# Three edits to a fused attention and two-expert-layer kernel: a written instruction order in the attention, gate products beside held-back products, and a gather in place of a scatter

## The chip, the core and the metric

The kernel runs on one core of one Trainium2 chip. The metric is the time of one execution on the device in microseconds (us). TensorE does matrix products and transposes, VectorE and ScalarE work elementwise on SBUF and PSUM, GpSimd does elementwise work and issues indirect DMAs, and SyncE issues most other DMAs. Semaphores order engines and queues; within one engine instructions start in the order of its stream.

## What is computed

The reference is three layers in a row (float32; 2 batches x 768 tokens = N = 1536 tokens, width D = 512, 8 experts, F = 1024):

```python
scores = q @ k.T / sqrt(64) - slope[h] * dist       # 8 heads of 64; per token its last 96 keys and 8 global ones
x = softmax(masked scores) @ v                      # -> (1536, 512)
P = sinkhorn(exp(x @ wg1 - max), 8 rounds)          # (1536, 8), rows and columns balanced
x2 = sum_e P[:, e] * (relu(x @ w1[e]) @ w2[e])      # all experts for all tokens
order = argsort(-(x2 @ wg2))                        # greedy: best (token, expert) pairs first,
assign each token to one expert, 192 per expert     # a full expert takes no more
out[t] = relu(x2[t] @ v1[e(t)]) @ v2[e(t)]          # its one expert only
```

## The kernel before

**Precision.** Large products are done in float16 with each operand split into a high and a low half, so one product is three matmuls (`mm3`, L710 to L712; `held_back`, L833). A split is a scaled copy on ScalarE (L618, L703) and a subtraction on VectorE (L619, L705). Scales are powers of two from a maximum over the matrix. Attention is float32.

**Attention** (`band_attention`, L350 to L582). Twelve blocks of 128 tokens, each in two units of four heads, 24 units. Per block, `start` loads q and k, turns them on TensorE (L440, L445) and copies the turned halves out of PSUM on ScalarE (L442, q) and VectorE (L447, k). Per unit: `weigh` makes scores (L465), adds the bias table and takes the maximum on VectorE (L471), the exponential and its sum on ScalarE (L474), and normalises on GpSimd (L481); `turn` transposes the weights (L491) and copies them (L494 VectorE, L496 ScalarE); `mix` multiplies by the values (L510). After a block's two units, `split_x` splits the result and makes the gate's logits. The loop at L536 traces unit t with the transposes of t - 1 and the value products of t - 2; behind them, from block 6 on, it places one hidden product of expert 0 per step. Beside it `early` (L699) loads expert 0's two weight matrices and splits them. The tables of distances start from `iota` on GpSimd (L87, L389). Tracing order is not the final order here: the scheduler sets each engine's stream from dependencies and priorities.

**The expert layer** (L789 to L943). For each expert: hidden = relu(x w1) per block of 512 tokens, then the second product. The second products of six (expert, token block) pairs, `post` (L914), are kept back: `held_back` is a generator of 192 steps (over all six) of three matmuls, `pin`ned to program order, which fills TensorE during the routing. Each time eight steps are done, one block of 128 tokens of `acc` (the layer's output) has got its last or next term, on ScalarE and GpSimd (L838, L839), or on VectorE for the last pair (L841). The second gate's logits `L` come in parts, and the last part of the last expert, `late_logits(7, tb)` for the three token blocks, stands behind all hidden products (L943): twelve groups of 16 narrow matmuls (`gate_product`, L138, L139) with one PSUM tile, each followed by two small operations on VectorE (L144, L145).

**The routing** (L1007 to L1086). Seven rounds: `propose` (L978 ff.) gives each token its best expert, masks of who is ahead of whom are made in twelve pieces (L1043, L1046 on VectorE, three pieces on ScalarE), counted on TensorE in three groups of 12 matmuls (L1051), and the 192nd proposal of each expert sets a bound under which others are masked out. `run(n)` places n held steps; a round has 7, then 4, 8 and 2 behind the three groups, then 3 and 3: 27. The steps left over come out in `finish(held)` after the last proposal.

**Handover** (L1087 to L1172). The slot of each token is counted (`si`, L1102). Twelve indirect DMAs (L1122) scatter the twelve blocks of `acc`, with the token's number as a 513th column, to their slots in `xg` in HBM; `load_rows` loads 384 sorted rows for a pair of experts with four SyncE DMAs, and `turn_rows` transposes and splits them (L1175, L1177). The scale over all tokens uses an all-reduce on GpSimd (L102) once `on_pool` is set. `fetch` (L1151) loads an already split 2 MB weight matrix of the second layer into a buffer that has come free; the first five are traced ahead of the row loads, two more under `tc.issue_after(st.ins)`, which places their issue behind the last row load on its engine.

Of the kernel before, what the change touches and what calls it, by code (L numbers as in the profile page):

```python
# [40 lines left out]
def tile_sparse_attention_moe_moe(ctx, tc, q, k, v, ng, nl, wg1, w11, w12, wg2, w21, w22, out, taps=None):  # L41
# [47 lines left out]
    nc.vector.tensor_scalar(ident, jp, 0.0, None, op0=ALU.is_equal)  # L89
# [44 lines left out]
    def gate_product(hi, lo, hl, n, f, dst, plus=None):  # L134

        pg = misc([P, 2 * E], name="pg")
        for c in range(n):
            nc.tensor.matmul(pg, hi(c), hl[:, c, 0:2].rearrange("p a e -> p (a e)"), start=c == 0, stop=False)  # L138
            nc.tensor.matmul(pg, lo(c), hl[:, c, 1:3].rearrange("p a e -> p (a e)"), start=False, stop=c == n - 1)  # L139
# [19 lines left out]
    gw1 = load_gate(wg1, "wg1")  # L159

    def attention(atp, aps):

        qtz = []
# [186 lines left out]
    def band_attention(atp, aps):  # L350


        order = [(b, i) for b in range(B) for i in range(NBLK)]
        NB = len(order)
        HU = HP // 2
# [14 lines left out]
        def load(n):  # L370
            if n >= NB:
                return
            qbs[n] = rows(q, n, "qb", 3)
            kbs[n] = rows(k, n, "kb", 3)
            b, i = order[n]
            if i:
# [7 lines left out]
        def table(own_only):  # L384
# [4 lines left out]
            nc.gpsimd.iota(rel[:, 0:P], pattern=[[-1, P]], base=0, channel_multiplier=1,  # L389
                           allow_small_or_imprecise_dtypes=True)  # L390
            if not own_only:
                nc.gpsimd.iota(rel[:, P:wl], pattern=[[-1, NP]], base=NP, channel_multiplier=1,
                               allow_small_or_imprecise_dtypes=True)
            m = atp.tile([P, W], F32, name=f"keep{W}")
# [11 lines left out]
            eng = nc.vector if own_only else nc.gpsimd  # L406
            for h in range(H):
                eng.tensor_scalar(tb[:, h, :], rel, 2.0 ** (-8.0 * (h + 1) / H), NEG, op0=ALU.mult, op1=ALU.min)
            tabs.append(tb)

        scales, vams = {}, {}

        def magnitude(n):

            b, i = order[n]
            if i == 0:
                vams[b] = sml.tile([P, NBLK + 1], F32, name="vam")
            nc.vector.tensor_reduce(vams[b][:, i:i + 1], vos[n], axis=AX.XY, op=ALU.max, apply_absolute_value=True)

        def batch_scale(b):  # L420

            am = vams.pop(b)
            nc.vector.tensor_reduce(am[:, NBLK:], am[:, :NBLK], axis=AX.X, op=ALU.max)
            s = pow2_scale(am[:, NBLK:], "sv", bufs=2)
            f = sml.tile([P, 1], F32, name="gf")
            nc.vector.tensor_mul(f, s[:, 1:2], gw1[1][:, 1:2])
# [3 lines left out]
        slabs, kgs = {}, {}  # L430

        def start(n):

            b, i = order[n]
            S = SimpleNamespace(n=n, b=b, i=i, W=WB if i else P, nch=2 if i else 1, ex={}, et={}, pa=None)
            S.cks = [P, NP + ng][:S.nch]
            qb, kb = qbs.pop(n), kbs.pop(n)
            pt = aps.tile([P, HP, P], F32, name="pq", tag="tr", bufs=2)
            for p in range(HP):
                nc.tensor.transpose(pt[:, p, :], qb[:, 2 * p:2 * p + 2, :].rearrange("p h d -> p (h d)"), ident)  # L440
            S.qt = atp.tile([P, HP, P], F32, name="qt", bufs=2)
            nc.scalar.activation(S.qt, pt, AF.Copy, scale=qs)  # L442
            pt = aps.tile([P, HP, P], F32, name="pk", tag="tr", bufs=2)
            for p in range(HP):
                nc.tensor.transpose(pt[:, p, :], kb[:, 2 * p:2 * p + 2, :].rearrange("p h d -> p (h d)"), ident)  # L445
            S.slab = slabs[n] = atp.tile([P, HP, WB], F32, name="slab", bufs=3)
            nc.vector.tensor_copy(S.slab[:, :, 0:P], pt)  # L447
# [3 lines left out]
            else:  # L451
                nc.gpsimd.tensor_copy(S.slab[:, :, P:P + NP], slabs.pop(n - 1)[:, :, P - NP:P])
                nc.gpsimd.tensor_copy(S.slab[:, :, P + NP:], kgs[b])
            S.vs = [vos[n]] + ([vps.pop(n)] if i else [])
            return S

        def weigh(S, u):

            W = S.W
            ex = S.ex[u] = atp.tile([P, 2, 2, WB], F32, name="ex", bufs=3)  # L460
            st = sml.tile([P, 4, 4], F32, name="st4", bufs=4)
            ps = [aps.tile([P, 2, 256], F32, name=f"ps{j}", tag=f"sc{j}", bufs=1) for j in range(2)]
# [5 lines left out]
            for y in range(HU):  # L468
                for j in range(2):
                    z = 2 * y + j  # L470
                    nc.vector.tensor_tensor_reduce(ex[:, y, j, :W], ps[j][:, y, :W],  # L471
                                                   tabs[min(S.i, 1)][:, 2 * (HU * u + y) + j, :W], 1.0, BIG,
                                                   ALU.add, ALU.min, st[:, 0, z:z + 1])
                    nc.scalar.activation(ex[:, y, j, :W], ex[:, y, j, :W], AF.Exp, bias=st[:, 0, z:z + 1], scale=-1.0,  # L474
                                         accum_out=st[:, 1, z:z + 1])
# [8 lines left out]
        def turn(S, u):  # L484
            ex = S.ex.pop(u)
            ets = S.et[u] = []
            for a, ck in enumerate(S.cks):
# [4 lines left out]
                et = atp.tile([P, 2, 2, P], F32, name="et", bufs=5)  # L492
                if a:
                    nc.vector.tensor_copy(et[:ck], pe[:ck])  # L494
                else:
                    nc.scalar.activation(et[:ck], pe[:ck], AF.Copy)  # L496
                ets.append(et)
# [15 lines left out]
        def split_x(S):  # L513
# [5 lines left out]
            nc.scalar.activation(hi, S.pa, AF.Copy, scale=s[:, 0:1])  # L519
            nc.vector.scalar_tensor_tensor(lo, S.pa, s[:, 0:1], hi, op0=ALU.mult, op1=ALU.subtract)  # L520
            yield
            gate_product(lambda kc: xT[tb_i][:, 0, kc, tcol:tcol + P], lambda kc: xT[tb_i][:, 1, kc, tcol:tcol + P],
                         gw1[0], KC, f, logits[:, S.n, :])

        load(0)
        load_own(0)
        load(1)
        for n in range(1, NBLK + 1):
# [3 lines left out]
        blocks = {0: start(0)}  # L532
        table(True)
        units = [(n, u) for n in range(NB) for u in range(2)]
        splits = []
        for t in range(len(units) + 3):  # L536
            n, u = divmod(t, 2)
            if u == 0:
                load(n + 2)
                if n:  # L540
                    load_own(n + NBLK)
            for z, (c0, c1) in enumerate(((1, 6), (6, 11))):
                if c0 <= n < c1:
                    next(early[z], None)
                    next(early[z], None)
                if (n, u) == (c1, 0):
                    finish(early[z])
            for x in splits:
                next(x, None)
            if t < len(units):  # L550
                weigh(blocks[n], u)
            if t == 0:
                table(False)
            if t < 3:
                for i in (2 * t, 2 * t + 1):
                    if i < NBLK:
                        magnitude(i)
            if t == 2:
                for i in range(6, NBLK):
                    magnitude(i)  # L560
                batch_scale(0)
            if u == 1 and 1 <= n < NBLK:
                magnitude(NBLK + n - 1)
            if u == 0 and n + 1 < NB:
                blocks[n + 1] = start(n + 1)
            if (n, u) == (NBLK, 0):
                magnitude(2 * NBLK - 1)
                batch_scale(1)
            if 0 <= t - 1 < len(units):
                m, x = units[t - 1]  # L570
                turn(blocks[m], x)
            if 0 <= t - 2 < len(units):
                m, x = units[t - 2]
                mix(blocks[m], x)
                if x:
                    S = blocks.pop(m)
                    g = split_x(S)
                    next(g)
                    splits.append(g)
            if n >= 6 and first_hidden:  # L580
                hidden(*first_hidden.pop(0))
        while splits:  # L582
            finish(splits.pop(0))
# [39 lines left out]
    first_hidden = [(0, tb, [f]) for tb in range(NTB - 1) for f in range(FC)]  # L623
# [75 lines left out]
    early = [prep(0, 0, 4), prep(0, 1, 4)]  # L699

# [45 lines left out]
    else:  # L746
        with tc.tile_pool(name="att", bufs=1) as atp, tc.tile_pool(name="aps", bufs=1, space=PSUM) as aps:
            band_attention(atp, aps)
# [40 lines left out]
    for x in first_hidden:  # L789
        hidden(*x, steps=1)  # L790
    hidden(0, NTB - 1, steps=1)
    done.add(("hidden", 0))
    acc = lat.tile([P, NC, DM + 1], F32, name="acc", tag="acc", bufs=1)
# [473 lines left out]
```

## Time and profile before

| what | value |
|---|---|
| median of 3 runs | 1383.05 us (1382.59 to 1385.24) |
| the profiled execution's own time | 1383.23 us |
| its span | 1381.4 us |
| mean granted TensorE clock | 0.975 of 2.4 GHz |
| TensorE busy (matmuls) | 1305.9 us, 95% |
| TensorE weight loads | 671.6 us, 49% |
| VectorE, ScalarE, GpSimd busy | 816.1, 596.4, 162.6 us |

The span is from the first to the last instruction of the profiled execution. Busy time counts an engine's instructions; the clock is what the throttle granted, 1.0 being 2.4 GHz and 0.5 being 1.2 GHz. A row of the timeline gives the start, the time, the engine, the line of the source, the operation, the tile written and the tiles read, their shapes, the number of like instructions in a row, and in brackets the engine's idle time before it and what ended that.

### The profile page before, as it was taken

How to read it: one execution, taken by the hardware profiler on the slowest of the kernel's cores; microseconds unless marked ns; L12 is line 12 of the kernel's file. 1: busy time of each engine (PE TensorE's matmuls, PEld its weight loads, DVE VectorE, ACT ScalarE, POOL GpSimd, SP SyncE). 2: the span in 40 equal slices, each digit the busy share in tenths (PEclk: the TensorE clock that was granted, in tenths of full speed). 3: DMA queues.
4: the chain of work that ended last, by engine and by line, in shares of the span. 5: the costliest groups of instructions: out<-in, count | busy, mean ns of one | idle time of the engine just before them, and what ended most of it. 6: DMA issues, size and time to landing. Idle time of an engine off the chain costs nothing. (4 is left out here: it accounts for less than half of the span.)

```text
span 1381.4 us, 19879 instructions
## 1 busy us (share of the span) xinstructions
PE 1305.9 (95%) x7956; PEld 671.6 (49%) x7956; DVE 816.1 (59%) x1765; ACT 596.4 (43%) x1053; POOL 162.6 (12%) x259
## 2 busy tenths in 40 slices
PE   5899999999999999999999999999988999919998
PEld 3655544444444444444444444455544444407775
DVE  5787586666666666665665654466537878702121
ACT  3667541344253435324341632456534657403332
POOL 5233210000000000000000000010001434030000
PEclk8999999999999999999999999999998999959999
DMA  8352013526433624451462351130010223148740
GB/s 217 82 150 74 1 61 122 183 71 217 140 123 122 217 88 156 149 183 61 147 202 78 117 188 61 51 132 2 1 61 1 104 81 122 62 143 301 274 199 28
DMA packets 96748, 164.93 MB, mean 119 GB/s; under 512 B 50064, under 2 KB 50064, under 8 KB 94096
## 3 DMA queue, kind: packets, MB, share of 16 engines
q1 hardware_dynamic: 94448, 153.18, 33.3%
q0 software_dynamic: 2208, 10.49, 2.0%
q8 instruction: 62, 1.02, 0.3%
q14 instruction: 30, 0.25, 0.1%
HBM read 119.61 MB, written 44.05 MB: 118 GB/s over the span
## 5 line engine op out<-in xcount | busy, mean ns | idle before, releaser
L710 PE MATMUL ph<-xt,wslot 128*128 128x512 f16 x768 | 291.1, 379 | 0.1
L711 PE MATMUL ph<-xt,wslot 128*128 128x512 f16 x768 | 291.0, 379 | 0.0
L712 PE MATMUL ph<-xt,wslot 128*128 128x512 f16 x768 | 291.0, 379 | 0.0
L703 ACT ACTIVATE hslot<-ph 128x512 f16<-128x512 f32 x192 | 114.1, 594 | 253.7 <-PE ph L712 252.0
L710 PE MATMUL py<-wslot,hslot 128*128 128x512 f16 x576 | 218.3, 379 | 0.0
L711 PE MATMUL py<-wslot,hslot 128*128 128x512 f16 x576 | 218.3, 379 | 0.0
L712 PE MATMUL py<-wslot,hslot 128*128 128x512 f16 x576 | 218.3, 379 | 0.0
L705 DVE TENSOR_TENSOR hslot<-relu,hslot 128x512 f16<-128x512 f32 x192 | 132.2, 689 | 111.2 <-ACT relu L704 110.9
L665 DVE TENSOR_REDUCE wam<-raw 128x1 f32<-128x1024 f32 x120 | 143.9, 1212 | 29.8 <-DMA raw<-in_moe_w_dram 29.7
L618 ACT ACTIVATE spill<-raw,s 128x1024 f16<-128x1024 f32 x64 | 72.6, 1146 | 162.7 <-DVE inv L669 64.7
L833 PE MATMUL py<-wslot,hslot 128*128 128x512 f16 x576 | 132.1, 381 | 0.0
L704 ACT ACTIVATE relu<-ph 128x512 f32<-128x512 f32 (+1 forms) x224 | 129.3, 577 | 0.0
L712 PEld LDWEIGHTS <-wslot 128*128 128x128 f16 x768 | 75.1, 98 | 87.4
L710 PEld LDWEIGHTS <-wslot 128*128 128x128 f16 x768 | 75.1, 98 | 86.9 <-issue 2.4
L711 PEld LDWEIGHTS <-wslot 128*128 128x128 f16 x768 | 75.1, 98 | 85.3
L619 DVE SCALAR_TENSOR_TENSOR spill<-raw,s,spill 128x1024 f16<-128x1024 f32 x64 | 81.9, 1283 | 56.5 <-ACT spill L618 55.3
L618 ACT ACTIVATE wslot<-raw,s 128x1024 f16<-128x1024 f32 (+1 forms) x72 | 73.2, 1050 | 76.0 <-DVE s L114 76.0
L816 DVE SCALAR_TENSOR_TENSOR acc<-py,pf,acc 128x512 f32<-128x512 f32 x60 | 45.0, 750 | 84.8 <-PE py L712 84.8
L710 PEld LDWEIGHTS <-hslot 128*128 128x128 f16 x576 | 56.3, 98 | 68.0
L712 PEld LDWEIGHTS <-hslot 128*128 128x128 f16 x576 | 56.3, 98 | 68.0
L711 PEld LDWEIGHTS <-hslot 128*128 128x128 f16 x576 | 56.3, 98 | 67.9
L619 DVE SCALAR_TENSOR_TENSOR wslot<-raw,s,wslot 128x1024 f16<-128x1024 f32 (+1 forms) x72 | 82.8, 1160 | 10.9 <-ACT wslot L618 10.1
(249 smaller groups left out, 1677.3 us busy)
## 6 DMA issues: line engine op xcount, KB each, us to landing
raw<-in_moe_w_dram SPq DMA_DIRECT2D x64, 1024.0 KB, 6.6
ws<-spill SPq DMA_DIRECT2D x64, 512.0 KB, 3.1
w2slot<-ws SPq DMA_DIRECT2D x16, 2048.0 KB, 9.7
hd<-hslot POOLq DMA_DIRECT2D x2, 2048.0 KB, 6.9
hslot<-hd SPq DMA_DIRECT2D x2, 2048.0 KB
qb<-in_q_dram SPq DMA_DIRECT2D x12, 256.0 KB, 3.4
kb<-in_k_dram SPq DMA_DIRECT2D x12, 256.0 KB, 6.7
vo<-in_v_dram SPq DMA_DIRECT2D x12, 256.0 KB, 3.3
```

What stands on the lines that cost most here:

```text
L618: nc.scalar.activation(hi, raw, AF.Copy, scale=s[:, 0:1])
L619: nc.vector.scalar_tensor_tensor(lo, raw, s[:, 0:1], hi, op0=ALU.mult, op1=ALU.subtract)
L665: nc.vector.tensor_reduce(am[:, a:a + 1], part, axis=AX.X, op=ALU.max, apply_absolute_value=True)
L703: nc.scalar.activation(hi, ps, AF.Relu, scale=HS)
L704: latest["act"] = nc.scalar.activation(r[:, :n], ps, AF.Relu, scale=HS)
L705: latest["dve"] = nc.vector.tensor_sub(lo, r[:, :n], hi)
L710: nc.tensor.matmul(out_, lhs(0, a), rhs(0, a), start=a == 0, stop=False)
L711: nc.tensor.matmul(out_, lhs(0, a), rhs(1, a), start=False, stop=False)
L712: nc.tensor.matmul(out_, lhs(1, a), rhs(0, a), start=False, stop=a == n - 1)
L816: latest["dve"] = nc.vector.scalar_tensor_tensor(acc[:, c, :DM], ps, pf[:, c:c + 1], acc[:, c, :DM], op0=ALU.mult, op1=ALU.add)
L833: pin(nc.tensor.matmul(ps, h[:, y1, f, t * P:t * P + P], w[:, y2, f, :], start=f == 0 and n == 0, stop=f == FC - 1 and n == 2))
```

## The change

1. Identity and distance tables are built on VectorE (a ramp `colx` by doubling, its transpose `rowx`) and not by `iota`.
2. The attention is traced inside `in_order()`, which chains every instruction to the one traced before it on the same engine. The loop is rewritten step by step; q is turned and copied ahead of k; a product of expert 0 stands ahead of the step's transposes; VectorE and ScalarE exchange the two copies of the transposed weights. Expert 0's two matrices are split in eight parts each, and the low half of every second part is made by GpSimd.
3. `late_logits` of expert 7 for token blocks 0 and 1 are placed in the expert loop, behind the hidden block after them; those of block 2 are pinned and have one held step after each group.
4. `run` in a round: 8, then 3, 6 and 2, then 3 and 3: 25 steps.
5. `acc` has 512 columns and is stored in token order by twelve SyncE DMAs. The list of tokens by slot (`inv`) is made by comparing slots with a ramp and twelve small matmuls; `load_rows` is three indirect DMAs on GpSimd that gather by `inv`, which serves the final scatter too. The scale's all-reduce is the form that uses TensorE (`on_pool.clear()`).

```diff
-    jp = cst.tile([P, P], I32)
-    nc.gpsimd.iota(jp, pattern=[[1, P]], base=0, channel_multiplier=-1)
+    colx = cst.tile([P, P], F32)
+    nc.vector.memset(colx[:, 0:1], 0.0)
+    n = 1
+    while n < P:
+        nc.vector.tensor_scalar(colx[:, n:2 * n], colx[:, 0:n], float(n), None, op0=ALU.add)
+        n *= 2
...
+    def in_order():
+        traced = nc.cur_bb.bb.instructions
+        last = traced[-1]
+        yield
...
+        for i in traced[start:]:
+            if i.engine in before:
+                tc.add_manual_dep(i, before[i.engine].name,
+                                  mybir.DependencyInfo(mybir.DependencyClass.NoSync, mybir.DependencyReason.DATA),
+                                  reason="in_order")
+            before[i.engine] = i
...
+        def matrix(which):
...
+            for a, part in enumerate(parts):
+                hi, lo = hl[:, 0, a * q8:(a + 1) * q8], hl[:, 1, a * q8:(a + 1) * q8]
+                nc.scalar.activation(hi, part, AF.Copy, scale=s[:, 0:1])
+                if a % 2:
+                    nc.gpsimd.tensor_scalar(part, part, s[:, 0:1], 0.0, op0=ALU.mult, op1=ALU.add)
+                    nc.gpsimd.tensor_tensor(lo, part, hi, op=ALU.subtract)
+                else:
+                    nc.vector.scalar_tensor_tensor(lo, part, s[:, 0:1], hi, op0=ALU.mult, op1=ALU.subtract)
+                yield
...
+        for t in range(NU + 4):
...
+            if S:
+                scores(S, u)
+            block = None
+            if u and n + 1 < NB:
+                block = turn_block(n + 1)
+                next(block)
+            if 0 <= t - 2 < NU:
+                m, x = divmod(t - 2, 2)
+                mix(blocks[m], x)
...
+            for x in gates:
+                next(x)
+            pt = broadcast() if bcs and not gates else None
+            if evac is not None:
+                finish(evac)
+                evac = None
+            if first_hidden and (0, 0) in W and ...:
+                evac = first_products(*first_hidden.pop(0))
+                next(evac)
+            last = None
+            if 0 <= t - 1 < NU:
+                m, x = divmod(t - 1, 2)
+                last = turn(blocks[m], x)
+                next(last)
+            if block:
+                next(block)
+            for z in range(4):
+                if S:
+                    soften(S, u, z)
...
+            if S:
+                normalise(S, u)
+            if last:
+                finish(last)
...
+            if t >= 4:
+                for _ in range(2):
+                    if next(weights, None) == "wait":
+                        break
...
+                         fc, L[:, c, :], plus=L[:, c, :], keep=beside is not None)
+            if beside:
+                beside(1)
...
-            if e == E - 1 and tb == 0:
-                gate_of_expert(e)
+            if e == E - 1:
+                if tb == 0:
+                    gate_of_expert(e)
+                else:
+                    late_logits(e, tb - 1)
...
-    for tb in range(NTB):
-        late_logits(E - 1, tb)
...
+    late_logits(E - 1, NTB - 1, run)
...
-        run(7)
+        run(8)
...
-                run((4, 8, 2)[c // 4])
+                run((3, 6, 2)[c // 4])
...
+    nc.vector.tensor_tensor(onep[:, :h6], sp[:, :h6, None].to_broadcast([P, h6, P]),
+                            ramp[:, None, :].to_broadcast([P, h6, P]), op=ALU.is_equal)
...
+    run(6)
+    pi = misc([P, NC], name="pinv")
+    for c in range(NC):
+        pin(nc.tensor.matmul(pi, onep[:, c, :], onea[:, c, :], start=c == 0, stop=c == NC - 1))
+    inv = lcs.tile([P, NC], I32)
+    nc.vector.tensor_scalar(inv, pi, 0.0, float(NT - 1), op0=ALU.max, op1=ALU.min)
     finish(held)
...
+    on_pool.clear()
     sx2 = pow2_scale(xam[:, NC:], "sx2")
...
     for c in by_time:
-        st = nc.gpsimd.indirect_dma_start(out=xg, out_offset=bass.IndirectOffsetOnAxis(ap=si[:, c:c + 1], axis=0),
-                                          in_=acc[:, c, :], in_offset=None)
...
+        nc.sync.dma_start(xg[c * P:c * P + P, :], acc[:, c, :])
...
-        nc.sync.dma_start(xr[:, 0, :], xg[r0:r0 + P, :])
...
+        for z in range(3):
+            st = nc.gpsimd.indirect_dma_start(out=xr[:, z, :], out_offset=None, in_=xg,
+                                              in_offset=bass.IndirectOffsetOnAxis(ap=inv[:, 3 * a + z:3 * a + z + 1],
+                                                                                  axis=0))
```

## Rows read from the trace of the kernel before

**Rows 1.** Busy time by stretches, their sum over 0 to 165 us, by engine.

```profile
sum 165.00, PE 141.60 PEld 91.80 DVE 112.73 ACT 98.26 POOL 62.20; mean PE 47.20 PEld 30.60 DVE 37.58 ACT 32.75 POOL 20.73
```

**Rows 2.** Timeline of TensorE and VectorE, gate products: start, time, instruction, idle and releaser.

```profile
1027.89 0.17 PE L138 MATMUL pg<-vg7hl,hslot 128*128 128x16 f16 x1
...
1029.02 0.18 PE L138 MATMUL pg<-vg7hl,hslot 128*128 128x16 f16 x1 [0.58 <-DVE L L145]
...
1029.41 0.17 PE L139 MATMUL pg<-vg7hl,hslot 128*128 128x16 f16 x1
...
1042.05 0.25 DVE L980 TENSOR_REDUCE rw<-L 128x12 f32<-128x96 f32 x1
```

**Rows 3.** Stretches: length, busy time by engine, granted clock, DMA share, GB/s.

```profile
1033.00:1042.00 9.00, 4.41 (x121) 3.68 (x118) 4.56 (x22) 0.00 (x0) 0.00 (x0) 0.50 0.22 88
1042.00:1047.00 5.00, 4.64 (x18) 3.36 (x19) 3.60 (x12) 2.35 (x3) 0.26 (x1) 0.55 0.00 0
```

**Rows 4.** Timeline of four engines, routing and handover.

```profile
1127.39 54.45 SPq L1151 DMA_DIRECT2D w2slot<-ws  x4
...
1205.79 0.25 DVE L980 TENSOR_REDUCE rw<-L 128x12 f32<-128x96 f32 x1
...
1217.95 0.38 POOL L102 PARTITION_ALL_REDUCE amax<-xam  x1 [6.65 <-issue]
1218.52 1.20 POOL L1122 DMA_INDIRECT xg<-acc,si  x1 [0.20 <-issue]
...
1238.86 0.90 PE L1175 MATMUL px<-ident,raw 128*128 128x128 f32 x3 [30.24 <-DMA raw<-xg]
...
1241.99 0.48 PE L710 MATMUL ph<-xt,w2slot 128*128 128x192 f16 x2 [0.24 <-ACT xt L1177]
```

**Rows 5.** Timeline, start and end of the attention.

```profile
8.03 0.23 POOL L87 IOTA jp<- 128x128 int32 x1 [7.59 <-issue]
...
11.84 0.89 PE L465 MATMUL ps<-slab,qt 64*128 64x128 f32 x8
...
164.56 0.39 PE L510 MATMUL pa<-et,vp 104*64 104x128 f32 x4
```

**Rows 6.** Groups by line, 0 to 170 us: instructions, busy time, mean ns, idle before.

```profile
L481 POOL TENSOR_SCALAR ex<-ex,st 128x232 f32<-128x232 f32 x80 | 39.2, 508 | 55.4 <-DVE st L477 22.3 <-ACT xt L519 18.1 <-PE pe L491 10.4
L474 ACT ACTIVATE ex<-ex,st 128x232 f32<-128x232 f32 x80 | 38.1, 478 | 15.0 <-DVE st L471 14.9
L471 DVE CUSTOM_DVE_ANT_0 ex<-ps,tab 128x232 f32<-128x232 f32 x80 | 27.9, 393 | 5.3 <-PE ps L465 5.3
...
L496 ACT ACTIVATE et<-pe 128x512 f32<-128x512 f32 x24 | 14.1, 589 | 10.8 <-PE pe L491 10.6
...
L619 DVE SCALAR_TENSOR_TENSOR wslot<-raw,s,wslot 128x512 f16<-128x512 f32 x16 | 11.7, 742 | 0.0
```

**Rows 7.** Timeline of TensorE and VectorE, last counts of a round.

```profile
1078.64 5.35 PE L833 MATMUL py<-wslot,hslot 128*128 128x512 f16 x24
...
1082.51 0.34 DVE L1046 SCALAR_TENSOR_TENSOR xt<-raw,rw,tie 128x128 bf16<-128x128 f32 x1
...
1083.93 0.83 PE L1051 MATMUL pr<-xt,Bz 128*32 128x512 bf16 x12
```

**Rows 8.** DMA issues of four stretches: KB each, us from issue to landing.

```profile
xg<-acc,si POOLq DMA_INDIRECT x12, 4.5
...
w2slot<-ws SPq DMA_DIRECT2D x2, 2048.0 KB, 14.5
...
raw<-xg SPq DMA_DIRECT2D x1, 128.2 KB, 8.6
...
out_dram<-spill,idx POOLq DMA_INDIRECT x1, 8.2
```

**Rows 9.** Timeline of GpSimd, two additions of 128x512.

```profile
1143.22 7.21 POOL L839 TENSOR_TENSOR acc<-acc,relu 128x512 f32<-128x512 f32 x1 [3.98 <-ACT relu L838]
...
1151.83 1.09 POOL L839 TENSOR_TENSOR acc<-acc,relu 128x512 f32<-128x512 f32 x1 [1.41 <-ACT relu L838]
```

More of the change, by code (lines that the diff above doesn't have):

```diff
@@ L158, in tile_sparse_attention_moe_moe @@
     SX = [SXA[:, c, :] for c in range(NC)]
-    gw1 = load_gate(wg1, "wg1")
+    @contextmanager
+    def in_order():
+        traced = nc.cur_bb.bb.instructions
+        last = traced[-1]
+        yield
+        start = next(k for k in reversed(range(len(traced))) if traced[k] is last) + 1
+        before = {}
+        for i in traced[start:]:
[4 more added lines that the diff above has]
+            before[i.engine] = i
     def attention(atp, aps):
+        gw1 = load_gate(wg1, "wg1")
         qtz = []
@@ L368, in load_own, with load_qk, load_past @@
                 vos[n] = rows(v, n, "vo", 8)
[L370 to L376, printed above, removed]
+        def load_qk(n):
+            if n < NB:
+                qbs[n] = rows(q, n, "qb", 3)
+                kbs[n] = rows(k, n, "kb", 3)
+        def load_past(n):
+            if n < NB and order[n][1]:
+                b, i = order[n]
                 t = atp.tile([P, H, D], F32, name="vp", bufs=3)
@@ L531, in band_attention @@
         nc.scalar.activation(warm, ones[:, 0:1], AF.Exp)
-        blocks = {0: start(0)}
         table(True)
-        units = [(n, u) for n in range(NB) for u in range(2)]
-        splits = []
-        for t in range(len(units) + 3):
+        finish(turn_block(0))
+        weights = matrices()
+        next(weights)
+        fresh, gates = [], []
+        evac = None
+        magnitudes = {0: (0,), 1: (1, 2), 2: (3, 4), 3: (5,)}
+        magnitudes.update({t: (t - 2,) for t in range(8, 8 + NBLK)})
@@ L537, in band_attention @@
+        mixed = []
+        for t in range(NU + 4):
             n, u = divmod(t, 2)
+            S = blocks.get(n) if t < NU else None
             if u == 0:
-                load(n + 2)
+                load_qk(n + 3)
                 if n:
[L541 to L551, printed above, removed]
+                    load_past(n + 1)
+                load_own(n + 6)
+            if S:
[7 more added lines that the diff above has]
+                mix(blocks[m], x)
+                if x:
+                    mixed.append(blocks.pop(m))
@@ new lines, in band_attention @@
+            for x in gates:
[3 more added lines that the diff above has]
+                finish(evac)
+                evac = None
+            if first_hidden and (0, 0) in W and all(c in split for c in range(first_hidden[0][1] * CPB,
+                                                                             first_hidden[0][1] * CPB + CPB)):
+                evac = first_products(*first_hidden.pop(0))
+                next(evac)
@@ L558, in band_attention @@
[L558 to L583, printed above, removed]
+                nc.vector.tensor_scalar(jp, colx, rowx, None, op0=ALU.subtract)
@@ L586, in tile_sparse_attention_moe_moe @@
+        if evac is not None:
+            finish(evac)
+        for x in gates + fresh:
+            finish(x)
+        finish(weights)
     pools = {}
@@ L622, in tile_sparse_attention_moe_moe @@
     hs = {}
-    first_hidden = [(0, tb, [f]) for tb in range(NTB - 1) for f in range(FC)]
+    first_hidden = [(0, tb, f) for tb in range(NTB - 1) for f in range(FC)]
     def view(t, which):
@@ L941, in tile_sparse_attention_moe_moe, with all_held, run @@
     finish(flow)
-    for tb in range(NTB):
-        late_logits(E - 1, tb)
+    for n, (e, tb) in enumerate(post):
+        if (e, tb) in away:
+            m = n - len(post) + len(away)
+            get_back(e, tb, NTB * post[m][0] + post[m][1])
+    def all_held():
+        for e, tb in post:
+            yield from held_back(e, tb, (e, tb) != post[-1])
+    held = all_held()
+    def run(n):
+        for _ in range(n):
+            next(held, None)
+    late_logits(E - 1, NTB - 1, run)
     if "L" in taps:
@@ L987, in propose @@
         return w
-    for n, (e, tb) in enumerate(post):
-        if (e, tb) in away:
-            m = n - len(post) + len(away)
-            get_back(e, tb, NTB * post[m][0] + post[m][1])
-    def all_held():
-        for e, tb in post:
-            yield from held_back(e, tb, (e, tb) != post[-1])
-    held = all_held()
-    def run(n):
-        for _ in range(n):
-            next(held, None)
     NQ = NT // 512
```

304 lines of the change are left out of this document (215 added, 89 removed).

## The prediction

> **What bounds the kernel now.** I read the stretches of the first 165 us, then the long middle, then the handover from the routing to the second set of experts. From 200 to 1000 us TensorE is busy without a hole, and the change touches nothing there. What can move lies in three places.
>
> First the attention. TensorE is marked busy for 141.6 of the first 165 us, but its weight loads for only 91.8; VectorE has 112.7 us of work, ScalarE 98.3 [rows 1]. No engine is full: the stage is held by the chain score product, score reduction (VectorE), exponential (ScalarE), normalising (GpSimd), transpose, copy, value product, and by who stands in whose queue. By the busy row at most 165 - 141.6 = 23 us can be gained here, by the weight loads up to 73. The Trainium skill (Trainium Kernel Development and Optimization, Performance Expectations) says that matmul busy time is a bad measure of the distance to the roofline and LDWEIGHTS busy a good one; the gap between 141.6 and 91.8 agrees. By it the upper bound would be 73; I need neither end for the sum.
>
> Second the gate products between expert 7's last hidden block and the first round. They start at 1027.89 right behind the last hidden product, each group of 16 waits some 0.6 us for VectorE to empty the one bank, and round 1 starts at 1042.05 [rows 2]: 14.1 us for 12 groups, 1.17 each. From 1033 to 1042 the granted clock was 0.50 (1.2 GHz), after TensorE had been half busy since 1028, and from 1042 to 1047 it was still 0.55 [rows 3].
>
> Third the handover. Round 8's proposal starts at 1205.79; TensorE then waits 30.24 us until the first sorted rows have landed, and the first expert product starts at 1241.99 [rows 4]: 36.2 us from proposal to product. In that gap GpSimd sits idle 6.65 us ahead of its all-reduce, then issues eleven scatters one behind the other, and SyncE loads only after the last.
>
> **The change part by part.** All sums are made against the profiled run, 1383.23 us (span 1381.4 and 1.8 outside it); the median of three is 1383.05, so the two are the same here.
>
> *Attention in written order.* (a) Start: the identity no longer waits for GpSimd's iota at 8.03, VectorE makes it from some 15 small operations. The first q and k blocks are now the first loads. The first scores then start when those blocks are there and turned; I put that at 7.5 instead of 11.84 [rows 5], 4.3 earlier; bounds 0 and 8 (all that GpSimd's start held). (b) A step without expert products (t = 0 to 13): VectorE has four reductions (0.39 each, 1.6), a copy of the transposed weights (0.6), half a key copy and half a split per step (0.7), two normalising operations (0.4), and weight maxima, magnitudes and logits of about 1.2; it also waits some 0.7 for the fourth exponential [rows 6]. That is 5.2 a step, 73 us for 14. (c) A step with a product (t = 14 to 23): ScalarE has two passes of the product before (1.2), four exponentials (1.9), one copy (0.6), half a query copy and half a split (0.6) and up to two weight pieces (0.7 on average), 5.0 together [rows 6]; and it stands idle some 1.3 while VectorE subtracts that product and reduces the first scores, since both now come in one written queue. 6.3 a step, 63 for ten. (d) Four steps that only drain, 4.6 each: 18. Together 7.5 + 73 + 63 + 18 = 162 with 13 products of expert 0 done. Before, the last value product starts at 164.56 [rows 5], also with 13 done. **3 us less.** Half of the weight splits go from VectorE to GpSimd. Nothing shows such a queue here; bounds: 20 less (the written order closes most of the 23) and 36 more (the last rival). I take the small value since steps before and after have nearly the same work.
>
> *Gate products.* Token block 0's four groups now stand ahead of the hidden block 2 in the trace and can be set between its products: a group's 16 products take 0.4 us from the first to the last [rows 2], 1.6 in all. Block 1's four come after it, as bare as now: 4 x 1.17 = 4.7. Block 2's four have three products of a held-back block between them (0.67, by 5.35 for 24 [rows 7]), which fill the 0.58 wait but don't shorten the chain: 4.7. Until round 1: 1.6 + 4.7 + 4.7 = 11.0 instead of 14.1: **3 less**, and 4 of the 192 held steps are done besides. Bounds: 0 (block 0's groups don't fit in) to 7 (block 1's also do).
>
> *The clock after it.* From 1042 to 1047 TensorE did 4.6 us of work at 0.55 [rows 3]; at 1.0 that is some 2.3. With the held products between, TensorE is about 90% busy from 4.7 us on. **2 less**; bounds 0 (the clock falls as before) and 2.5.
>
> *25 steps a round.* The held products ahead of a round's last counts go from 24 to 18. TensorE ended it at 1083.93 while VectorE's last mask had been done at 1082.85, 1.1 earlier [rows 7]. The slack in the seven rounds, read in the same way, is 2.0, 1.1, 1.1, 1.1, 0.9, 0.9, 1.3; six products are 1.3, so they bring 1.3, then 1.0, 1.0, 1.0, 0.8, 0.8, 1.2: **7 less**, after which the masks end each round. The step more at the head of the round (0.65) is taken back by the step less behind it. Bounds 4 to 9 (seven times 1.3). The steps taken out are not saved work: they come back in the handover, where TensorE had nothing.
>
> *Handover.* Counted from round 8's proposal. Slots at +3.8 as now. Then masking, a copy, two compares of 128x768 (0.95 each, a little over the 0.74 of a 512-wide row [rows 6]), two small ones, one accumulator update: +7; 12 products of 12 columns and the conversion: the token list is there at +7.6. Six held steps lie beside that, five more end at +10.6, the last accumulator block is ready at +11.5 and has to be stored, since the gathers read all twelve blocks. The all-reduce with its 6.65 and eleven scatters are gone. What is late next is that last store. Two weight loads of 2 MB were kept behind the row loads by being queued after them on SyncE; the row loads are now GpSimd's, the call that queues behind them acts on GpSimd alone, so nothing holds these loads. Their buffers come free with the last held product, +10.6, a microsecond before the store can go. They go first in SyncE's queue. Two such loads landed 14.5 us after the issue, and a load of 128 KB issued 3 us behind one landed after 8.6, about when that one had [rows 8]. So the store lands at +26, gathers are issued at +26.2, 27.5 and 28.7 (1.2 each as the scatters [rows 4]), land 4.5 later as the scatters did [rows 8], and transposes and split take 1.8: +35 instead of +36.2. **1 less.** Bounds: +25 (nothing in the way: store in 4.5, third gather at +18.5, 4.5 to land) and +39. By the Trainium skill (DMA: Bandwidth & Descriptors, Queues, rings and completion order) descriptors of one issuing engine are taken in ring order, while rows of several engines take turns; by that the store stays behind the loads, and if it were ahead the gathers would share with them. The 8.6 us row agrees with the first half.
>
> Behind the first product the order of work is as before. Sum: 3 + 3 + 2 + 7 + 1 = 16, **1383.2 - 16 = 1367 us.**
>
> **Rivals.**
> *The store goes first.* If SyncE's order has the last store ahead of the two loads, it lands at +16; the gathers run beside 4 MB, where a scatter took 8.2 us [rows 8] rather than 4.5: third gather +18.5, landed +26.7, product at +28.5. 6.5 us less than the forecast: **1360**. For it: the store stands first in the program. Against: four such loads went out from 1127.39 on [rows 4], in the middle of the rounds and far ahead of the place where they are used.
> *The fixed order stalls.* Before, a late operation let another one pass; in a written queue everything behind it waits. If each of the 24 full steps costs 0.4 more than counted, the attention is 9.6 longer, 7 over now: **1377**. For it: five queues wait on each other in each step. Against: ScalarE and VectorE have a third or more of their time free [rows 1].
> *Slower: GpSimd's weight splits.* GpSimd is to do eight subtractions of 128x512 in front of the normalising that the next transposes wait for. Such an addition took 1.09 us, but 7.21 beside VectorE's work [rows 9]. At 7.2 a step holds 4 x 0.51 of normalising [rows 6], 8.3 of split and 0.4: 10.7 instead of 6.3, eight times: 35 more, **1402**. It decides from about 4 us for a subtraction on. Against: GpSimd's normalising passes in the attention take 0.51 each with VectorE at work beside them all the time [rows 1, 6].
> *It doesn't do what it says:* if TensorE's own work and not the slack set the rounds, the moved steps give nothing and the gap alone shrinks: 1383 - 9 = 1374, inside the range.
>
> **How the numbers follow.** Forecast 0.53, store first 0.23, stalling order 0.13 (with the last case), GpSimd 0.09, other 0.02. Range: 1350 (store first, and 10 us more out of the attention, within its bound) to 1379. What a measurement can't tell from no change here is 0.2%, 2.8 us. Faster by more: 0.88, the first three less a little; within: 0.03; slower: 0.09, GpSimd's case.
>
> **What the profile would show.** First scores near 7.5 and the last value product near 160, with GpSimd's subtractions near 1.1 us; round 1 starting some 11 us behind the last hidden product at a clock of 1.0; the last count of a round following VectorE's last mask, not 18 held products; two 2 MB loads issued ahead of the last 256 KB store, TensorE idle for 23 us at clock 0.5. A store that lands 3 us after its issue would make the handover wrong, steps of 7 us or more the attention.

## The result and the profile after

The changed kernel takes 1364.17 us (median of 4 runs, 1363.08 to 1367.52) where the kernel before took 1384.07 (1382.59 to 1385.24): a ratio of 0.9861, 95% interval 0.984 to 0.9882. The forecast was 1367, the range 1350 to 1379. The profiled execution has a span of 1362.6 us, 18.8 less, at a mean granted clock of 0.988.

The total came out near the forecast, but its terms did not. Marks read from the two timelines, in us:

| from, to | before | after | difference | forecast |
|---|---|---|---|---|
| start to the end of expert 0's 20th hidden product | 183.69 | 175.81 | -7.9 | -3 |
| from there to round 1 (gate products) | 858.4 | 856.9 | -1.4 | -3 |
| rounds 1 to 6 | 140.2 | 134.4 | -5.8 | -8 with the clock |
| round 7 | 23.5 | 28.1 | +4.5 | -1 |
| round 8's proposal to the first product of the sorted rows | 36.2 | 27.1 | -9.1 | -1 |
| from there to the end of the last scatter's issue | 135.7 | 136.7 | +1.0 | 0 |

Three terms are far off: the attention and the handover, which gave 4.9 and 8.1 us more than forecast, and round 7, which came out 5.5 worse. Their errors largely cancel.

Attention. The timeline of after, first scores and last value product; [rows 5] had 11.84 and 164.56.

```profile
7.38 1.22 PE L579 MATMUL ps<-slab,qt 64*128 64x128 f32 x8 [0.88 <-DVE slab L568]
...
148.86 0.39 PE L637 MATMUL pa<-et,vp 104*64 104x128 f32 x4
```

The groups by line, 0 to 170 us (count, then busy time and mean ns of one), where L605 answers to L481 of [rows 6]:

```profile
L605 POOL TENSOR_SCALAR ex<-ex,st 128x232 f32<-128x232 f32 x80 | 36.5, 475 | 59.0 <-DVE st L601 24.9 <-PE pe L616 17.7 <-ACT et L622 15.3
...
L535 POOL TENSOR_TENSOR wslot<-raw,wslot 128x512 f16<-128x512 f32 x8 | 9.3, 1157 | 0.7
L534 POOL TENSOR_SCALAR raw<-raw,s 128x512 f32<-128x512 f32 x8 | 7.0, 872 | 1.7 <-ACT wslot L532 1.7
```

GpSimd's new subtractions take 1.16 us, and its normalising is no slower (0.475 for 0.508): the slower rival is out. The sum of the stretches, to be held against [rows 1], shows VectorE with 127.5 us of work in the first 165 where it had 112.7:

```profile
sum 165.00, PE 136.20 PEld 91.34 DVE 127.52 ACT 98.52 POOL 68.34; mean PE 45.40 PEld 30.45 DVE 42.51 ACT 32.84 POOL 22.78
```

Gate products. Stretches of after (length, busy time of TensorE, its loads, VectorE, ScalarE, GpSimd, granted clock, DMA share, GB/s), where [rows 3] had 0.50 and 0.55:

```profile
1022.00:1027.00 5.00, 2.48 (x75) 2.11 (x72) 3.05 (x13) 0.96 (x2) 0.00 (x0) 0.84 0.81 292
1027.00:1033.00 6.00, 5.89 (x62) 2.75 (x59) 2.38 (x11) 0.00 (x0) 0.00 (x0) 0.57 0.26 109
1033.00:1038.00 5.00, 4.96 (x29) 3.02 (x30) 4.86 (x14) 3.96 (x5) 0.26 (x1) 1.00 0.00 0
```

The clock still falls behind the bare groups of token block 1, but now it is low during the held products (0.57) and back at full speed when round 1 starts at 1032.73, as forecast. The low clock has a price that the prediction did not count. From 1027 to 1032 it was 0.50, one held step lasted 1.44 us, and a group with its step 1.71, not 1.17:

```profile
1026.90 1.44 PE L1027 MATMUL py<-wslot,hslot 128*128 128x512 f16 x3
...
1028.61 1.44 PE L1027 MATMUL py<-wslot,hslot 128*128 128x512 f16 x3
```

Round 7. Rows of GpSimd, VectorE, ScalarE and TensorE in after:

```profile
1174.81 6.12 POOL L1033 TENSOR_TENSOR acc<-acc,relu 128x512 f32<-128x512 f32 x1 [4.19 <-ACT relu L1032]
...
1179.47 0.34 DVE L1245 SCALAR_TENSOR_TENSOR xt<-raw,rw,tie 128x128 bf16<-128x128 f32 x1
...
1180.97 0.63 ACT L927 ACTIVATE absj<-acc 128x512 bf16<-128x512 f32 x1 [5.30 <-POOL acc L1033]
...
1182.67 1.01 PE L1250 MATMUL pr<-xt,Bz 128*32 128x512 bf16 x5 [3.93 <-ACT xt L1239]
```

GpSimd's addition lasts 6.12 us, as one did in [rows 9], and ends 1.1 us after VectorE's row of masks breaks off at 1179.81. ScalarE has the absolute maximum of that very block next in its queue and stands for 5.30; its masks for the third count are behind it; TensorE waits 3.93 for them. None of this was in the prediction.

Handover. Rows of after, where [rows 4] had the scatters:

```profile
1195.21 0.25 DVE L1195 TENSOR_REDUCE rw<-L 128x12 f32<-128x96 f32 x1
...
1205.22 0.32 SPq L1367 DMA_DIRECT2D w2slot<-ws  x1
1206.01 0.32 SPq L1342 DMA_DIRECT2D xg<-acc  x1
1206.38 0.86 SPq L1367 DMA_DIRECT2D w2slot<-ws  x1
...
1214.78 1.19 POOL L1377 DMA_INDIRECT raw<-xg,inv  x1 [14.79 <-issue]
...
1222.31 0.80 PE L903 MATMUL ph<-xt,w2slot 128*128 128x192 f16 x4 [0.24 <-ACT xt L1391]
```

One 2 MB load goes 0.8 us ahead of the last store (issued at +10.8, forecast +11.5), the other right behind it, and the gathers begin 8.8 us after the store's issue, not 14.5.

### The profile page after: what moved, and what is told of

Its sections match the earlier page's. It is cut to its first block, busy times and chain, and to the rows that moved or that the text cites. A ratio compares the mean times of both kernels' runs of the same rounds, so it can differ in the third digit from the quotient of the medians.

```text
span 1362.6 us, 19963 instructions
## 1 busy us (share of the span) xinstructions
PE 1296.3 (95%) x7969; PEld 668.5 (49%) x7969; DVE 827.7 (61%) x1790; ACT 592.9 (44%) x1049; POOL 169.1 (12%) x264
## 4 chain that ended last, share of the span: by engine, by line
PE 73%; issue 9%; DVE 8%; ACT 5%; POOL 3%; DMA 1%; POOLq 0%; DVEq 0%; ACTq 0%
PE ph L903 12%; PE ph L905 12%; PE ph L904 12%; PE py L904 9%; PE py L903 9%; PE py L905 9%; PE py L1027 3%; ACT ex L594 2%; POOL acc L1033 2%; DVE xt L1242 1%; DVE xt L1244 1%; POOL out_dram L1346 1%; DVE et L624 1%; PE pg L150 1%; DVE xt L1245 1%
## 5 line engine op out<-in xcount | busy, mean ns | idle before, releaser
L898 DVE TENSOR_TENSOR hslot<-relu,hslot 128x512 f16<-128x512 f32 x192 | 135.4, 706 | 112.2 <-ACT relu L897 111.5
L813 ACT ACTIVATE wslot<-raw,s 128x1024 f16<-128x1024 f32 x56 | 62.5, 1145 | 77.4 <-DVE s L125 76.7
L113 POOL PARTITION_ALL_REDUCE amax<-wam x30 | 10.5, 351 | 665.4 <-DVE wam L861 665.4
```

Source lines behind the costliest of these rows:

```text
L813: nc.scalar.activation(hi, raw, AF.Copy, scale=s[:, 0:1])
L898: latest["dve"] = nc.vector.tensor_sub(lo, r[:, :n], hi)
```

## The experiments

Each was measured together with the kernel before, in three groups. The kernel before had medians of 1385.4, 1387.0 and 1385.3 us in them (parts alone and `no_order`; the four from `abs_late` to `both`; the other four), so kernels are compared by their ratios to it, with 95% intervals in parentheses. Places in the kernel are compared by the marks of the table above.

### Each part alone

`only_attention` is before with points 1 and 2 of the change, `only_gather` with point 5, `only_gate_rounds` with points 3 and 4; their edits are those parts of the diff.

> The kernel before with the attention part alone (points 1 and 2 of the change). What the trace of after shows: expert 0's 20th hidden product ends at 175.81 instead of 183.69, and TensorE is without a hole from there to the last hidden product, so 7.9 us stay: 1383 - 8 = 1375. By the prediction's sum the part is worth 3: 1380. If the 8 us come from another part beside it: 1383.

Measured: 1374.79, ratio 0.9935 (0.9921 to 0.9948). The gain is the attention's and it stays.

> The kernel before with the store, the list by slot and the gather alone (point 5), 27 steps a round as before, so three held steps are left after the last proposal instead of eleven. The last block is ready some 3.5 us behind the proposal, not 11. If its store takes 8.5 us beside a 2 MB load, as in after, and the first product follows the first gather by 7.5: 3.6 + 8.5 + 7.5 = 20 us from proposal to product instead of 36.2, so 1383 - 16 = 1367. If the store goes ahead of the loads and lands in 3: the list is there at 7, product at 15, 1362. If the part is worth what the prediction said (1): 1382.

Measured: 1367.96, ratio 0.9878 (0.9863 to 0.9893). From proposal (1204.94) to first product (1225.17) it is 20.2 us, as the first case has it.

> The kernel before with the gate products beside others and 25 steps a round alone (points 3 and 4). Theory from the trace of after: gate products 1.3 less, rounds 1 to 6 together 5.8 less, and eight held steps more behind the last proposal, which put off the all-reduce and the eleven scatters by about 1.5: 1383 - 1.3 - 5.8 + 1.5 = 1377. If GpSimd's additions stall round 7 here as they do in after (5 us): 1382. By the prediction's sum (3 + 2 + 7 less, nothing lost behind): 1371.

Measured: 1380.63, ratio 0.9966 (0.9952 to 0.9979). Round 7 stalls here as well: 28.3 us, the others 21.8 to 22.8, while round 7 takes 23.6 in `only_attention` and 23.7 in `only_gather`. The stall belongs to points 3 and 4, not to the gather.

By the spans of the profiled executions the parts bring 10.0, 16.0 and 2.6, 28.6 together, where all at once bring 18.8 (by the medians 32.7 and 19.9). Most of the missing 9.8 lies in the handover: the gather alone takes 16.0 from it, in after only 9.1. There thirteen held steps stand behind the last proposal (192, less 4 beside the gate products, less 7 x 25), and the last store, which waits for them, goes out 10.8 us behind the proposal and not 3.7.

### What the written order does

`no_order` takes the chain away and keeps the new text; `order_tensor` keeps it for TensorE alone; `lo_vector` makes all low halves on VectorE.

```diff
-            with in_order():
-                band_attention(atp, aps)
+            band_attention(atp, aps)
```

> After, with the attention traced without the chain that fixes every engine's order; the text of the loop stays. Of the 7.9 us, 4.5 are there at the first score (7.38 for 11.84), before any order matters. If the written order brings the rest: 1364 + 3.4 = 1367.5. If the new sequence in the text does it and the chain is idle: 1364. If the chain costs (stalls in the queues): below 1363.

Measured: 1356.06, ratio 0.9794 (0.9781 to 0.9808). The third case, and a large one: the 20th product ends at 166.03, 9.8 us earlier than in after. The chain costs, and the new text alone is worth 17.7. These two figures are from one profile each. Over all profiles here the mark lies at 182.2 to 185.3 with the old attention (three), at 174.4 to 176.7 with the new text and the whole chain (six), and at 165.6 to 170.0 without it (three). By the means the text brings 16.5 and the chain takes 8.4 back.

```diff
-            if i.engine in before:
+            if i.engine in before and i.engine == mybir.EngineType.PE:
```

> After, with the chain kept on TensorE alone and the other engines free; TensorE's stream stays nearly as in after. Without any chain the time was 1356.1, with all of it 1364.2. If TensorE's fixed order is what costs: 1364. If it is the elementwise engines' written order: 1356. If it is both: between, about 1360.

Measured: 1353.70, ratio 0.9774 (0.976 to 0.9787), the 20th product at 163.34. So the cost is in the other queues; TensorE's written order costs nothing that can be seen. One place where it arises is ahead of the second unit's reductions. First after, rows of VectorE and ScalarE:

```profile
8.60 0.29 DVE L591 CUSTOM_DVE_ANT_0 ex<-ps,tab 128x128 f32<-128x128 f32 x1 [1.37 <-PE ps L579]
...
10.62 0.17 DVE L600 TENSOR_SCALAR st<-st 128x4 f32<-128x4 f32 x1 [1.08 <-ACT ex L594]
...
10.91 0.26 DVE L419 TENSOR_SCALAR rel<-colx,rowx 128x128 f32<-128x128 f32 x1
...
13.70 1.61 DVE L435 TENSOR_SCALAR tab<-rel 128x232 f32<-128x232 f32 x8
...
15.41 0.68 DVE L490 TENSOR_REDUCE vam<-vo 128x1 f32<-128x512 f32 x1
16.01 0.28 DVE L591 CUSTOM_DVE_ANT_0 ex<-ps,tab 128x128 f32<-128x128 f32 x1
...
16.33 0.40 ACT L594 ACTIVATE ex<-ex,st 128x128 f32<-128x128 f32 x1 [3.84 <-DVE st L591]
```

and the same work in the run with TensorE's chain alone:

```profile
6.22 0.27 DVE L423 TENSOR_SCALAR keep<-rel 128x224 f32<-128x224 f32 x1
...
8.50 0.43 DVE L432 TENSOR_TENSOR rel<-rel,keep 128x224 f32<-128x224 f32 x1
...
9.75 1.22 DVE L435 TENSOR_SCALAR tab<-rel 128x232 f32<-128x232 f32 x6
...
11.43 0.68 DVE L490 TENSOR_REDUCE vam<-vo 128x1 f32<-128x512 f32 x1
12.03 0.28 DVE L591 CUSTOM_DVE_ANT_0 ex<-ps,tab 128x128 f32<-128x128 f32 x1
...
12.68 0.39 ACT L594 ACTIVATE ex<-ex,st 128x128 f32<-128x128 f32 x1
```

In after, VectorE waits 1.37 us for the first scores and 1.08 for ScalarE's fourth exponential, and only then makes the distances (from 10.91) and the second table. Freely placed, most of the work on the distances (6.22 to 8.93) lies ahead of the first reduction and six of the table's eight pieces (L435, 9.75) fill the wait for the exponential. The second unit's reductions start 4.0 us earlier, at 12.03 and not at 16.01.

The loss is not spread evenly over the units. Scores of unit 6 in after, and in the run with TensorE's chain alone:

```profile
33.85 1.05 PE L579 MATMUL ps<-slab,qt 64*128 64x232 f32 x8
```

```profile
25.74 1.05 PE L579 MATMUL ps<-slab,qt 64*128 64x232 f32 x8
```

Units 7, 15 and 24 follow at 39.72, 77.80 and 134.26 in after, and at 34.51, 69.27 and 124.06 in the other. So 8.1 us are lost ahead of unit 6; from 8 to 34 us VectorE is busy for 19.8 of the 26 us in after, for 25.6 in the other. The next step gives 2.9 back, and the nine steps from unit 15 to unit 24, beside which hidden products run, lose only 1.7 more. The sums of waits from 8 to 150 us agree that VectorE and ScalarE wait longer for each other in after (waiter, releaser, total us, times, longest). After:

```profile
ACT ex L594 <- DVE st L591: 32.5, 23, 3.8
...
DVE st L600 <- ACT ex L594: 13.2, 23, 1.1
```

Without the chain:

```profile
ACT ex L594 <- DVE st L591: 24.2, 20, 3.4
...
DVE st L600 <- ACT ex L594: 7.0, 12, 1.1
```

In 23 of the 24 units VectorE stands for the exponential in after, in 12 without the chain. How much of the cost these waits make, beside those at the start, is not shown.

```diff
-                if a % 2:
+                if False:
                     nc.gpsimd.tensor_scalar(part, part, s[:, 0:1], 0.0, op0=ALU.mult, op1=ALU.add)
```

> After, with all sixteen low halves of expert 0's matrices on VectorE (eight more of 0.74 us there, and GpSimd rid of eight times 0.87 + 1.16). If VectorE, which is 78% to 90% busy until 90 us, carries the steps: 4 to 6 us slower, 1369. If GpSimd's splits ahead of its normalising hold the steps (the prediction's slower case, in small): 3 to 8 faster, 1358. If neither: 1364.

Measured: 1368.39, ratio 0.9879 (0.9864 to 0.9894), against 0.9861 (0.984 to 0.9882) for after: the intervals overlap, but the 20th product ends at 179.29, 3.5 us later and outside the 174.4 to 176.7 of the six profiles with after's attention. So GpSimd's share of the splits helps, by 3.5 of the 5.9 us that VectorE is spared (eight times 0.74), and the case in which it holds the steps up is out.

### What stalls round 7

```diff
+                last_act = nc.scalar.activation(rs[:, n * 512:n * 512 + 512], pr[n], AF.Copy)
...
+    with tc.issue_after(last_act.ins):
+        for c in by_time:
+            absmax_bound(acc[:, c, :], xam[:, c:c + 1], rsm)
```

> After, with the twelve absolute maxima of the finished blocks issued on ScalarE behind its last copy of round 7. In after one of them waits in round 7 for an addition on GpSimd that takes 6.12 us, ScalarE's masks stand behind it, and TensorE's counts wait 3.93 us; round 7 lasts 28.06 us, the others 22.0 to 23.0. Theory: round 7 falls to some 22.8, the maxima take 10 x 0.82 us and are done before the last block: 1364 - 5 = 1359. Rival: the masks wait for VectorE anyway, or the maxima now delay the scale: 1364 or more.

Measured: 1357.86, ratio 0.9795 (0.9782 to 0.9808). Round 7 is 23.0. Rounds 5 and 6 fall too, from 23.0 and 22.7 to 22.0 and 21.8, where in after the additions took 5.39 and 5.68 us. So the maxima in ScalarE's queue cost 6.9 us over the rounds of after, not 5. GpSimd's addition is as slow as before, only nobody waits for it:

```profile
1172.77 7.07 POOL L1033 TENSOR_TENSOR acc<-acc,relu 128x512 f32<-128x512 f32 x1 [4.12 <-ACT relu L1032]
...
1176.38 0.61 PE L1250 MATMUL pr<-xt,Bz 128*32 128x512 bf16 x8 [0.26 <-DVE xt L1245]
...
1178.57 1.36 DVE L1244 TENSOR_SCALAR xt<-raw,rw 128x128 bf16<-128x128 f32 x1
```

The last row is the other side of it: a mask piece of 128x128 that took 0.28 us in after's round 7 lasts 1.36, until the addition ends at 1179.84.

### What the store and the gathers wait for

`hold_sync` queues the two loads behind the last store on SyncE, `hold_gather` issues them from GpSimd behind the first six gathers.

```diff
-    with tc.issue_after(st.ins):
-        fetch_next(2)
+    with tc.issue_after(last_store.ins):      # hold_sync
+        fetch_next(2)
...
+    with tc.issue_after(st.ins):              # hold_gather
+        fetch_next(2, nc.gpsimd)
```

> After, with the two 2 MB loads queued on SyncE behind the last store of a block (one of them goes ahead of it in after). In after that store is issued at 1206.01 and the first gather starts at 1214.78, 8.5 us later. Theory (the store shares the DMA engines with the load issued 0.8 us ahead of it): the store lands in 3 to 4 us, the gathers then run beside both loads and take longer than their 3.8: product 2 to 5 us earlier, 1359 to 1362. Rival (the store's way to memory takes its 8.5 us in any case): 1364.

Measured: 1364.16, ratio 0.9845 (0.9831 to 0.9858), no better than after within the intervals. (By the rows of after its store took 8.8 us, not the 8.5 of the expectation.) Rows of it, timeline and DMA issues (us from issue to landing):

```profile
1206.05 0.89 SPq L1367 DMA_DIRECT2D w2slot<-ws  x2
...
1208.84 1.19 POOL L1377 DMA_INDIRECT raw<-xg,inv  x1 [9.22 <-DVE f L1354]
...
1222.10 0.80 PE L903 MATMUL ph<-xt,w2slot 128*128 128x192 f16 x4 [0.24 <-ACT xt L1391]
```

```profile
raw<-xg,inv POOLq DMA_INDIRECT x6, 8.8
```

> After, with the two 2 MB loads issued by GpSimd behind the first six gathers. The store lands in 3 to 4 us and the gathers have the DMA engines to themselves: product 5 us earlier, 1359, if the loads still come in time. If it is slower than the run with the loads behind the store, the loads are late for the second pair of experts; if it is faster by 2 or more, the gathers suffer from the loads there. Rival: 1364, nothing changes since the store takes 8.5 us in any case.

Measured: 1358.56, ratio 0.9795 (0.9782 to 0.9808).

```profile
1208.89 1.19 POOL L1377 DMA_INDIRECT raw<-xg,inv  x1 [9.14 <-DVE f L1354]
...
1216.58 0.80 PE L903 MATMUL ph<-xt,w2slot 128*128 128x192 f16 x4 [0.24 <-ACT xt L1391]
```

```profile
raw<-xg,inv POOLq DMA_INDIRECT x6, 3.7
```

Counted from the proposal, the gathers start some 5.6 us earlier in both than in after, so the store needs its 8.8 only behind a load: without one ahead of it the first gather starts 3.2 us after the store's issue. Its row names VectorE's L1354, done at 1208.03 in `hold_sync`, as what ended the wait, so 3.2 is a bound for the store from above. In `hold_sync` the gain is given back at once: six gathers beside 4 MB take 8.8 us, not 3.7. That is the mechanism of the rival "the store goes first", which put the product at +28.5; `hold_sync` has it at +27.3, `hold_gather` at +21.6. The Trainium skill (DMA: Bandwidth & Descriptors, Queues, rings and completion order) has descriptors of one issuing engine taken in ring order, while queues of several engines take turns; the store behind the load and the gathers beside it both agree.

### Together

> After, with both edits: the maxima behind the rounds and the two loads behind the gathers. They act in different stretches, so the gains add: 1364 - 10 = 1354. If the maxima, now close to the handover, delay the last block's store or the scale: 1357 to 1359.

Measured: 1351.29, ratio 0.9743 (0.973 to 0.9756). The two gains add.

> After without the chain, with the maxima behind the rounds and the loads behind the gathers. The chain's 8.1 us lie in the attention, the others' 12.9 behind 1160: they add, 1351.3 - 8.1 = 1343. If the attention's gain is given back behind it: 1351.

Measured: 1341.51, ratio 0.9690 (0.9676 to 0.9703). It adds too, and this version beats both kernels: without the chain, with the maxima behind the rounds and the loads behind the gathers.

> The same with 27 steps a round again (7 at the head, 4, 8 and 2 behind the counts). By the prediction's step 25 a round brings 7 us, so this is 7 slower: 1350. By the traces: a round grows by 0.8 (23.0 for 22.2), 5.6 in all; but no held step is left behind the last proposal, so the first gather waits for the list by slot alone and starts some 7.2 us behind the proposal instead of 13.9: 1343 + 5.6 - 6.7 = 1342, no difference that can be measured.

Measured: 1343.42, ratio 0.9695 (0.9682 to 0.9708): no difference that can be measured. Its seven rounds take 162.2 us where those of the version with 25 take 155.6, and its handover 15.6 for 21.5. First gather behind the proposal at 1178.17 with 25 steps:

```profile
1192.09 1.19 POOL L1377 DMA_INDIRECT raw<-xg,inv  x1 [9.14 <-DVE f L1354]
```

and behind that at 1189.15 with 27:

```profile
1197.12 1.19 POOL L1377 DMA_INDIRECT raw<-xg,inv  x1 [3.03 <-DVE inv L1325]
```

## Why the prediction was right, and where it was not

**The total** was right within its range, and so was the sign of every edit's term but round 7's. That it came within 3 us of the forecast is luck: the attention and the handover gave 4.9 and 8.1 us more than forecast, the gate products, rounds 1 to 6 and round 7 gave 1.6, 2.2 and 5.5 less.

**Attention.** The steps were sized well: the first score came at 7.38 (forecast 7.5), 14 steps without a product took 70.4 us (73), the ten with one 63.7 (63). What failed is "four steps that only drain": only two steps follow, by the last value product at 148.86 ten hidden products were done, not 13, and the other three followed bare at 2.6 us each. So 13 were done at 157.6 and not at 162, and the seven up to the 20th took 1.5 us less than before. Deeper, "steps before and after have nearly the same work" hid two large terms of opposite sign. The new text brings 17.7 us in one pair of profiles and 16.5 in the means (near the bound of 20 that the prediction kept), and the chain takes 9.8 or 8.4 back. That cost was there as the rival of the stalling order, 0.4 us a step or 9.6 in all; its sum came true, but as part of a larger gain and not evenly by steps. Which of the three elementwise queues carries most of it was not tried; VectorE's idle time at the start points to its queue. Which edit of the text brings most of the 17.7 stays open too, beyond the 4.5 at the start and the 3.5 of GpSimd's splits.

**Gate products.** From the last hidden product to round 1 it was 10.9 us, and the agreement with the forecast's 11.0 is luck: that sum held 1.6 for block 0's groups, which now lie among the hidden products, where about 1.7 is left for them. Counted with them, the part brought 1.4, not 3. The mis-sized term is the 4.7 of block 2. Block 1's bare groups took 4.8, as priced, but block 2's took 6.3 (1026.46 to 1032.73): its held products were priced at 0.67 as in [rows 7] and ran at a clock of 0.50, at 1.44. That the clock is back for round 1 came out as said: round 1 lasted 22.5 us for 25.7.

**25 steps a round.** Between versions without the stall, 25 against 27 steps change the rounds by 6.6 us (7 forecast, its mechanism as described). That the steps taken out "come back in the handover, where TensorE had nothing" is the step that failed: once the gather had shortened the handover, held work was its longest wait, and 5.9 of the 6.6 were given back. And a queue that the prediction never looked at, ScalarE's, put a maximum that waits for GpSimd ahead of its masks: round 7 came out 4.5 longer than before, and with rounds 5 and 6 that queue cost 6.9.

**Handover.** The mechanism was right in kind: the loads, no longer held on SyncE, get in the store's way. Its size was off because both loads were put ahead of the store. The row taken for it, 14.5 us for two loads issued together, stands for a store behind both; here one load went 0.8 us ahead of the store and the other right behind it, and the store took 8.8. So the order that ran lies between the forecast's (+35) and that of the rival in which the store goes first (+28.5), and the measured +27.1 is near the rival's time.

## What to carry to other kernels

Sum a queue's waits together with what stands behind them: an order written out for every engine can turn a short wait into lost time on the busiest one, here most of all in the first units, while the same text with only TensorE's order kept was at least as fast as any other form. Work moved out of one gap is free only if the gap that receives it has nothing else to do, so parts that fill and parts that shorten the same gap are not to be added. When a transfer changes its issuing engine, look at everything that its old queue was holding back.

## What was not expected of the hardware

An addition of 128x512 on GpSimd took 1.1 to 1.3 us alone and up to 7.1 beside VectorE's row of masks, nine such pieces making it 4.2 and fifteen 7.1. It ends about 1.1 us after VectorE pauses, and in `abs_late` VectorE's next piece lasts 1.36 for 0.28. It looks as if the addition got no turn while the pieces came one behind the other, and as if the piece behind them then stood for the whole addition; that is read from these rows, and no run tried it. The Trainium skill (SBUF — State Buffer, SBUF: two separate sides) describes an exclusive port that the two engines share and that one of them holds for a whole instruction. The long piece agrees with it.

Six gathers of 128 rows took 3.7 us from issue to landing without 2 MB loads beside them and 8.8 with two; the first gather started 3.2 us after the issue of the last 256 KB store where the loads came behind that store, and 8.8 where one had gone 0.8 us ahead.
